# Clustered attention and a rational MoE layer: what the clock-keeping products of TensorE read, and where the float16 identity is formed

## The chip, the cores and the metric

The kernel runs on one core of a Trainium2 chip. The metric is the device time of one execution in microseconds, and less is better. Five engines work side by side, each through a queue of its own in order: PE (TensorE, matrix products), DVE (VectorE), ACT (ScalarE), POOL (GpSimd) and SP (SyncE), whose queue issues the DMA transfers. PEld is the loading of PE's weights, which overlaps its products.

## The reference

For 4 batches of 8 heads with 768 positions of 64 values, q and k are assigned to the nearest of 16 centroids of their head, and attention runs only between positions of one cluster. The attention's output, 3072 rows of 512, goes through a layer with a rational function between two products:

```
q_assign = argmax(q_n . c_n);  k_assign = argmax(k_n . c_n)
scores = where(q_assign == k_assign, scale * q @ k.T, -1e9)
x = softmax(scores) @ v                    # 3072 x 512
h = x @ w_in                               # 512 x 2048
g = (a0 + a1 h + a2 h^2 + a3 h^3) / (1 + |b0| |h| + |b1| h^2 + 1e-6)
out = g @ w_out                            # 2048 x 512
```

## The kernel before

float32 operands are split into a high and a low float16 part, and the products are made of these parts. Per batch the kernel prepares pairs of heads (`prep`), runs the attention (`attend`, for the first pair of the first batch `attend_keys`, which keeps scores transposed), and then the layer (`moe`) over blocks of 256 rows. The weights are loaded and split once, in blocks of 512 columns or rows (`weights`). The work of one batch's attention is interleaved with the layer of the batch before.

Every operation of these functions is first recorded, and then emitted in the order of a long list of numbers in the file (`ORDER`). Within each engine's queue this order stands as it is written. What is not recorded but called directly, the constants at the head of the kernel (L372 to L401), is placed by the framework's scheduler: each engine's queue is filled with what it takes to be ready, so that such an instruction can stand behind recorded ones.

These lines matter here:

- L372 and L373 form `ident`, the float32 identity of 128x128, on GpSimd with `make_identity` (a memset and an affine select). `ones` (L374), `cq`, `tiny`, `up`, `eps` (L387) and `mrow` (L392 to L395) are memsets on DVE, `w16` and `pick` are formed on GpSimd.
- L389 and L390 form `ident16`, the float16 identity, as a cast of `ident` on DVE.
- `warm` (L781 to L788) records one group of eight products of `ident16` with itself into a PSUM tile that nothing reads. `K["warm"]` is 16, so there are 16 such groups; the list puts ten of them at the head of PE's queue, one more ahead of the first real step, and the other five between later steps.
- `prep` works on one pair of heads: ACT sums the squares of k and of q (`sumk`, `sumq`, L409 is the line of every activation), PE transposes the sums into a row (`kt`, `qt`, L1013), DVE takes the maximum (`km`, `qm`, L1015), PE spreads it over the partitions with `ones` (`kb`, `qb`, L1017), DVE makes powers of two of it (`ksc`, `qsc`, L1027 to L1070), ACT scales k and q into float16 (`tk`, `tq`) and DVE forms their low parts (L1089).
- `ident16` is also the identity of the transposes of `tk` and `tq` on PE (L980, the first pair of heads or pairs of the first batch), and of a smaller transpose in `attend_keys` (L1452).
- Loads go through SP's queue in order (L423). A load waits until its buffer's last reader is done: the raw weight blocks (`rwi`, `rwo`) and the first loads of v (`rvm`) share two buffers, k and q (`rk`, `rq`) have their own.

```python
ident16 = cp.tile([P, P], F16, name="ident16")
nc.vector.tensor_copy(out=ident16, in_=ident)
...
def warm(vt):
    wm = misc([P, 2 * TW], F32, f"warm{vt}")
    def spin():
        for _ in range(8):
            nc.tensor.matmul(wm.ap[:, :P], lhsT=ident16, rhs=ident16, start=True, stop=True)
    op("PE", 433, spin, [], [wm], vt)
```

Of the kernel before, what the change touches and what calls it, by code (L numbers as in the profile page):

```python
# [12 lines left out]
BF16 = mybir.dt.bfloat16  # L13
# [5 lines left out]
P = 128  # L19
# [23 lines left out]
class Plan:  # L43
# [5 lines left out]
    def op(self, eng, ns, fn, r=(), w=(), vt=0.0, claim=(), co=(), chain=None, n=None):  # L49
        self.ops.append(fn)  # L50
# [208 lines left out]
def clustered_attention_moe_kernel(  # L259
# [12 lines left out]
    nc = tc.nc  # L272
# [22 lines left out]
    def pool(name, space=None):  # L295
        if name not in pools:
            kw = {} if space is None else {"space": space}
            pools[name] = ctx.enter_context(tc.tile_pool(name=name, bufs=1, **kw))
        return pools[name]

    cp = pool("const")
# [45 lines left out]
    def misc(shape, dt, name):  # L347
        return bank(shape, dt, "m", name, NM)
# [22 lines left out]
    ident = cp.tile([P, P], F32, name="ident")  # L371
# [15 lines left out]
    nc.vector.memset(eps, 1e-9)  # L387

    ident16 = cp.tile([P, P], F16, name="ident16")  # L389
    nc.vector.tensor_copy(out=ident16, in_=ident)  # L390
    mrow = cp.tile([P, NCL], F16, name="mrow")
    nc.vector.memset(mrow, 0.0)  # L392
    nc.vector.memset(mrow[:, 0:8], M_BIG)
# [387 lines left out]
    def warm(vt):  # L781
        wm = misc([P, 2 * TW], F32, f"warm{vt}")

        def spin():
            for _ in range(8):
                nc.tensor.matmul(wm.ap[:, :P], lhsT=ident16, rhs=ident16, start=True, stop=True)

        op("PE", 433, spin, [], [wm], vt)  # L788

# [1064 lines left out]
```

## Time and profile before

| | |
|---|---|
| median of 3 runs | 903.31 us (903.31 to 904.04) |
| the profiled execution | 900.24 us |
| its span, first to last instruction | 898.4 us |
| mean granted TensorE clock | 0.99 of full |
| busy share of PE, DVE, ACT, POOL | 96%, 90%, 88%, 59% |

The rows come from one profiled execution. Times are microseconds from the start of the span, unless marked ns. A row of the timeline gives start, duration, engine, line, operation, what is written and read (a buffer's number is left out, so `ident16` appears as `ident`), how many instructions are merged, and in brackets how long the engine was idle before and what ended that. The chain of work that ended last is followed back from the last instruction, at each step to what released it or to the instruction ahead of it on its engine. The granted clock is 1.00 at 2.4 GHz and 0.50 at 1.2 GHz.

### The profile page before, as it was taken

The page shows a single profiled execution, that of the slowest core. Times are in us where ns is not written, and L with a number is a line of the kernel's source. Part 1 is how long each engine was busy: PE and PEld are TensorE (multiplying, and loading weights), DVE is VectorE, ACT ScalarE, POOL GpSimd, SP SyncE. Part 2 cuts the span into 40 slices and gives each one's busy share as a digit, 9 for nine tenths or more (in the row PEclk, how much of TensorE's full clock was granted, in tenths as well). Part 3 has the DMA queues.
Part 4 walks back from the last instruction along what each step waited for, and adds up shares of the span by engine and source line. Part 5 has one row for each costly group of instructions (what it writes and reads, how often), then busy time and mean ns, then how long its engine had stood idle before and what let it go on. Part 6 is the DMA issues. An engine that isn't in the chain of part 4 may idle for free.

```text
span 898.4 us, 20920 instructions
## 1 busy us (share of the span) xinstructions
PE 862.0 (96%) x7893; PEld 594.4 (66%) x7893; DVE 811.3 (90%) x1610; ACT 794.5 (88%) x1497; POOL 533.2 (59%) x530
## 2 busy tenths in 40 slices
PE   5699999988999999999999999999999999999998
PEld 4566777765666666657667666667676666767654
DVE  3999989789999999989999999999999998877793
ACT  4688899999999999999999999999999999895652
POOL 2337645677766385547556737565666555687664
PEclk9799999999999999999999999999999999999999
DMA  4698876779877999886979999989789875150000
GB/s 155 190 251 216 198 186 144 206 146 210 160 139 139 191 198 183 190 161 127 216 153 167 178 189 171 159 169 179 152 154 170 156 139 95 36 95 1 24 24 24
DMA packets 353013, 135.76 MB, mean 151 GB/s; under 512 B 327824, under 2 KB 344208, under 8 KB 352912
## 3 DMA queue, kind: packets, MB, share of 16 engines
q1 hardware_dynamic: 352912, 134.42, 74.0%
q8 instruction: 62, 1.02, 0.4%
q14 instruction: 39, 0.32, 0.1%
HBM read 41.98 MB, written 6.29 MB: 54 GB/s over the span
## 4 chain that ended last, share of the span: by engine, by line
PE 61%; DVE 17%; ACT 14%; issue 5%; POOL 1%; DMA 1%; SPq 1%; ACTq 0%; DVEq 0%
PE po L1761 20%; PE ph L1612 19%; PE s L1243 7%; PE px L1323 5%; DVE s L1272 3%; ACT s L409 3%; DVE ah L1303 3%; ACT u L409 2%; ACT ah L409 2%; PE s L1386 2%; PE z L1480 2%; PE px L1501 2%; DVE t L1637 1%; DVE t L1630 1%; PE ptl L1138 1%
## 5 line engine op out<-in xcount | busy, mean ns | idle before, releaser
L1612 PE MATMUL ph<-x,win 128*128 128x256 f16 x2304 | 266.2, 273 | 1.1 <-DVE t L1637 0.6
L1761 PE MATMUL po<-wout,g 128*128 128x512 f16 x1152 | 267.1, 379 | 0.0
L1612 PEld LDWEIGHTS <-win 128*128 128x128 f16 x2304 | 223.9, 98 | 42.0 <-DVE t L1637 2.9
L1761 PEld LDWEIGHTS <-g 128*128 128x128 f16 x1152 | 110.5, 98 | 120.1 <-issue 3.4
L1750 POOL TENSOR_TENSOR g<-t,u 128x512 f16<-128x512 f32 x84 | 112.7, 1344 | 93.8 <-DVE t L1743 56.6
L1677 POOL TENSOR_TENSOR s<-s,u 128x512 f32<-128x512 f32 x84 | 111.2, 1329 | 74.9 <-ACT s L409 73.1
L1272 DVE TENSOR_SCALAR_CACHE_REDUCE s<-s,cc 128x768 f32<-128x768 f32 x144 | 144.9, 1018 | 4.4 <-PE s L1243 3.5
L1303 DVE SCALAR_TENSOR_TENSOR ah<-s,su,ah 128x768 f16<-128x768 f32 x144 | 144.1, 1010 | 4.4 <-ACT ah L409 3.9
L409 ACT ACTIVATE ah<-s,su 128x768 f16<-128x768 f32 x144 | 127.8, 899 | 6.6 <-DVE su L1291 6.1
L409 ACT ACTIVATE s<-s,nm 128x768 f32<-128x768 f32 x144 | 125.6, 872 | 8.4 <-DVE s L1272 6.5
L1243 PE MATMUL s<-sk,sq 128*128 128x384 f16 x576 | 115.6, 327 | 6.3 <-DVE ah L1303 5.6
L1243 PEld LDWEIGHTS <-sq 128*128 128x128 f16 x576 | 52.0, 98 | 49.9 <-DVE ah L1303 16.4
L1323 PE MATMUL px<-at,vhi 128*64 128x256 f16 x864 | 73.9, 275 | 1.9 <-DVE s L1731 1.8
L409 ACT ACTIVATE t<-ph,gk 128x512 f32<-128x512 f32 x84 | 65.3, 778 | 0.0
L1630 DVE SCALAR_TENSOR_TENSOR t<-ph,gk,t 128x512 f32<-128x512 f32 x84 | 62.2, 742 | 2.5 <-ACT t L409 1.4
L1637 DVE SCALAR_TENSOR_TENSOR t<-t,gk,ph 128x512 f32<-128x512 f32 x84 | 62.3, 741 | 1.2
L409 ACT ACTIVATE u<-s,cq 128x512 f32<-128x512 f32 x84 | 59.8, 721 | 3.0 <-POOL s L1677 2.9
L409 ACT ACTIVATE s<-u,g 128x512 f32<-128x512 f32 x84 | 60.3, 723 | 0.5
L409 ACT ACTIVATE u<-ph,gk 128x512 f32<-128x512 f32 x84 | 57.7, 688 | 3.3 <-PE ph L1612 3.1
L1731 DVE SCALAR_TENSOR_TENSOR s<-s,g 128x512 f32<-128x512 f32 x84 | 59.8, 714 | 0.5
L1323 PE MATMUL px<-at,vlo 128*64 128x256 f16 x432 | 59.7, 273 | 0.0
L1323 PEld LDWEIGHTS <-vhi 128*64 128x64 f16 x864 | 45.0, 110 | 15.3 <-issue 10.3
(241 smaller groups left out, 1552.4 us busy)
## 6 DMA issues: line engine op xcount, KB each, us to landing
rwi<-in_moe_w_in_dram SPq DMA_DIRECT2D x16, 512.0 KB, 3.9
rwo<-in_moe_w_out_dram SPq DMA_DIRECT2D x16, 512.0 KB, 4.3
rk<-in_k_dram SPq DMA_DIRECT2D x32, 192.0 KB, 3.9
rq<-in_q_dram SPq DMA_DIRECT2D x32, 192.0 KB, 3.7
rvm<-in_v_dram SPq DMA_DIRECT2D x16, 384.0 KB, 4.0
rv<-in_v_dram SPq DMA_DIRECT2D x16, 384.0 KB, 4.1
out_dram<-ob SPq DMA_DIRECT2D x24, 256.0 KB, 2.9
sq<-sq SPq DMA_DIRECT2D x12, 192.0 KB, 4.1
```

Of the source, the lines that this page charges most:

```text
L409: lambda: nc.scalar.activation(out=out(), in_=in_(), func=func, **{a: (x() if callable(x) else x) for a, x in kw.items()}),
L1243: nc.tensor.matmul(sc.ap[:, i, :SH], lhsT=st["q" + x].ap[:, j, t, :], rhs=st["k" + x].ap[:, j, ks, :].rearrange("p t c -> p (t c)"), start ...
L1272: lambda nm=nm, view=view: ts(out=view(), in0=view(), scalar1=cc.ap[:, 0:1], scalar2=None, op0=ALU.mult, op1=ALU.min, accum_out=nm.ap),
L1303: lambda part=part, view=view, su=su: stt(out=part(1), in0=view(), scalar=su.ap, in1=part(0), op0=ALU.mult, op1=ALU.subtract),
L1323: nc.tensor.matmul(px.ap[j * D : (j + 1) * D, :], lhsT=vv.ap[:, j, kt, :], rhs=at[j].ap[:, p_, kt].rearrange("p t c -> p (t c)"), start=(i ...
L1612: nc.tensor.matmul(ph.ap[:, fi * TW : (fi + 1) * TW], lhsT=win[:, wpart, c, f * P : (f + 1) * P], rhs=xs[c].ap[:, xpart], start=(i == 0), ...
L1630: lambda t=t, h=h, ph=ph, col=col: stt(out=t[h].ap, in0=ph.ap, scalar=col("rho")(), in1=t[h].ap, op0=ALU.mult, op1=ALU.mult),
L1637: lambda t=t, h=h, ph=ph, col=col: stt(out=t[h].ap, in0=t[h].ap, scalar=col("a1")(), in1=ph.ap, op0=ALU.add, op1=ALU.mult),
L1677: lambda uv=uv, sv=sv: nc.gpsimd.tensor_tensor(out=sv(), in0=sv(), in1=uv(), op=ALU.mult),
L1731: lambda sv=sv, g16=g16: stt(out=sv(), in0=sv(), scalar=1.0 + 1e-6, in1=g16(0), op0=ALU.add, op1=ALU.mult),
L1750: lambda tv=tv, uv=uv, g16=g16, e=(nc.vector if kshare("gld", b, i_) else nc.gpsimd): e.tensor_tensor(out=g16(1), in0=tv(), in1=uv(), op=A ...
L1761: nc.tensor.matmul(po[ti].ap, lhsT=g16(gg)[:, c0 : c0 + P], rhs=wout[:, wpart, f, :], start=(i == 0 and f == 0), stop=(i == 2 and f == NF ...
```

## The change

The float16 identity is formed directly on GpSimd, with a memset and an affine select of its own, in place of the cast on DVE. A new constant tile of 128x128 bfloat16 ones is set by a memset on DVE, and the groups of eight products read it for both operands. The number, shape and order of the groups stay the same.

```diff
@@ -387,7 +387,9 @@
     nc.vector.memset(eps, 1e-9)
 
     ident16 = cp.tile([P, P], F16, name="ident16")
-    nc.vector.tensor_copy(out=ident16, in_=ident)
+    make_identity(nc, ident16)
+    w16w = cp.tile([P, P], BF16, name="w16w")
+    nc.vector.memset(w16w, 1.0)
     mrow = cp.tile([P, NCL], F16, name="mrow")
@@ -783,7 +785,7 @@
         def spin():
             for _ in range(8):
-                nc.tensor.matmul(wm.ap[:, :P], lhsT=ident16, rhs=ident16, start=True, stop=True)
+                nc.tensor.matmul(wm.ap[:, :P], lhsT=w16w, rhs=w16w, start=True, stop=True)
```

## Rows read from the trace of the kernel before

**Rows 1.** Stretches: length, busy PE, PEld, DVE, ACT, POOL, clock, DMA share, GB/s.

```profile
9.20:15.90 6.70, 6.69 (x89) 6.57 (x89) 0.00 (x0) 1.24 (x5) 2.98 (x4) 1.00 0.27 88
...
45.00:90.00 45.00, 43.91 (x471) 29.91 (x469) 43.02 (x107) 39.35 (x73) 24.40 (x26) 0.98 0.96 232
```

**Rows 2.** The chain that ended last, at its start: start, length, what.

```profile
8.32 0.69 DVE wwo L565
9.01 0.15 DVE ident L390
...
9.21 1.03 PE warm-39.99_113 L786 x8
...
12.78 0.45 PE warm-39.92_156 L786 x8
...
15.46 0.45 PE warm-39.86_234 L786 x8
```

**Rows 3.** DVE's waits from 0 to 45: in total, times, longest.

```profile
DVE km L1015 <- PE kt L1013: 6.9, 1, 6.9
```

**Rows 4.** Timeline, the constants at the head of GpSimd's and DVE's queues.

```profile
0.73 0.20 POOL masks.py:197 MEMSET ident<- 128x128 f32 x1 [0.29 <-POOLq L1838]
...
0.83 0.17 DVE L374 MEMSET ones<- 128x128 f32 x1 [0.83 <-PEq L1838]
...
1.08 0.29 POOL masks.py:199 TENSOR_SCALAR_AFFINE_SELECT ident<-ident 128x128 f32<-128x128 f32 x1
...
1.14 0.06 DVE L387 MEMSET eps<- 128x1 f32 x1
```

**Rows 5.** Timeline, ACT's sums of k and q and what follows them.

```profile
9.02 0.19 ACT L409 ACTIVATION_READ_ACCUMULATOR tk<-rk 128x1 f32 x1
...
10.00 0.19 ACT L409 ACTIVATION_READ_ACCUMULATOR tq<-rq 128x1 f32 x1
...
10.10 0.42 ACT L409 ACTIVATE cn<-cn 128x1 f32<-128x1 f32 x2
```

**Rows 6.** Timeline, first steps behind the constant products on PE and ACT.

```profile
15.75 0.27 PE L1013 MATMUL kt<-ident,sumk 128*1 128x128 f32 x1
...
17.16 0.27 PE L1013 MATMUL qt<-ident,sumq 128*1 128x128 f32 x1
...
17.38 0.94 ACT L409 ACTIVATE tk<-rk,ksc 128x768 f16<-128x768 f32 x1 [6.87 <-DVE ksc L1045]
...
18.23 0.83 ACT L409 ACTIVATE rvm<-rvm 128x768 f32<-128x768 f32 x1
...
19.88 0.66 ACT L409 ACTIVATE mwi<-rwi 128x512 f32<-128x512 f32 x1
```

**Rows 7.** Timeline of SP's queue, two issues of loads.

```profile
6.44 0.39 SPq L423 DMA_DIRECT2D rvm<-in_v_dram  x1
9.08 10.42 SPq L423 DMA_DIRECT2D rwi<-in_moe_w_in_dram  x2
```

**Rows 8.** Stretches of 1.5 us, columns as in rows 1.

```profile
12.00:13.50 1.50, 1.50 (x24) 1.50 (x22) 0.00 (x0) 0.00 (x0) 0.18 (x1) 1.00 0.02 8
...
18.00:19.50 1.50, 0.73 (x10) 0.54 (x9) 1.21 (x6) 1.50 (x4) 0.00 (x0) 0.98 0.00 0
19.50:21.00 1.50, 1.02 (x10) 1.03 (x11) 1.50 (x3) 1.50 (x3) 0.00 (x0) 0.50 0.50 134
...
43.50:45.00 1.50, 1.50 (x32) 1.09 (x31) 1.50 (x3) 0.22 (x1) 1.50 (x2) 0.50 1.05 388
```

**Rows 9.** Timeline, GpSimd's first product.

```profile
9.19 1.27 POOL L574 TENSOR_TENSOR wwo<-wwo,gwo 128x512 f32<-128x512 f32 x1 [6.44 <-DVE ident L390]
```

**Rows 10.** Timeline of PE, three steps at different clocks.

```profile
26.38 0.37 PE L1013 MATMUL kt<-ident,sumk 128*1 128x128 f32 x1
...
41.00 0.81 PE L1386 MATMUL s<-sk,sq 128*128 128x384 f16 x4 [0.47 <-DVE top L1396]
...
43.14 1.27 PE L1386 MATMUL s<-sk,sq 128*128 128x384 f16 x4 [1.33 <-DVE top L1396]
```

## The prediction

> **What bounds the kernel now.** I began with the busy time by stretch [rows 1], whose columns are length, busy time of PE, PEld, DVE, ACT and POOL with instruction counts, granted clock, DMA share and GB/s. In the bulk of the kernel three engines are close to full: of the 45 us from 45 on PE is busy 43.91, DVE 43.02, ACT 39.35, and DMA stands at 0.96. Those stretches are not what the change touches. From 9.20 to 15.90 the picture is another one: PE is busy 6.69 of 6.70 us, while DVE does nothing at all and ACT 1.24 us of work. PE's work there is the constant products.
>
> Next the chain that ended last, at its start [rows 2]. It goes through DVE's L565, then through the cast of the identity (L390, done at 9.16), then through eleven groups of eight constant products, which end at 15.91. So the products are not beside other work here; they are the chain. Nothing reads what they make, but PE takes its queue in order, and behind them stands the first real step, the transpose `kt` of the sums of k (L1013). The waits say the same from the other side [rows 3]: DVE's maximum of that transpose waits 6.9 us for it.
>
> Why do the products begin at 9.21? Not because the identity is late: GpSimd had it finished at 1.08 + 0.29 = 1.37 [rows 4]. The cast stands late in DVE's own queue, right after L565 of the second weight block (8.32 + 0.69 = 9.01), which had waited for a load. DVE's memsets, which need no input, all ran near 1 us [rows 4]. The engine queue is therefore not the order of the program's text, and what has no input goes first.
>
> **The change, part by part.**
> *The products' operand.* They now wait for a memset of 128x128 on DVE instead of the cast. No row shows this memset in bfloat16; the 128x128 float32 one took 0.17 us, the 128x1 one 0.06 [rows 4]. I take 0.17, the nearer in size; the other end makes the sum 0.1 us smaller or nothing. Standing behind the memset of L387 (1.14) it ends at about 1.3. From the cast's end to the first product there were 0.05 us [rows 2], so the products begin at about 1.4 instead of 9.2.
>
> *The products themselves.* Count and shape stay. In the trace four groups ran to 12.78, that is 3.57 us or 0.89 each with the first one's latency, and seven to 15.91, 0.45 each [rows 2]: the half (1.2 GHz) and the full (2.4 GHz) level. (The clock column shows 1.00 for the whole stretch [rows 1]; the groups' length is the better witness.) With the same four and seven they take 6.70 us and end at 8.1. If the clock does not come up at all, eleven take 11 x 0.89 = 9.8 and end at 11.2. That is the bad end.
>
> *What is late next.* `kt` needs the sums of k, which ACT finishes at 9.02 + 0.19 = 9.21 [rows 5]; with the same 0.05 it starts at 9.26. In the trace it starts at 15.75 [rows 6]. The products are over 1.1 us earlier, so **the gain at this point is 15.75 - 9.26 = 6.49 us**, set by ACT's sum and no longer by the products. With the clock never up it is 15.91 - 11.2 = 4.7.
>
> *Does the rest move by the same 6.49?* Everything after `kt` is a chain of queue order and data, so it moves unless it meets something that stays. What stays is what began before 9.2. I check each in turn. `qt` stood at 17.16, moved 10.67; the sums of q are ready at 10.00 + 0.19 [rows 5, 6]. ACT's scaling of k stood at 17.38, moved 10.89; ACT's queue ahead of it ends with the pair of 10.10 at 10.52 [rows 5, 6]. The square of v (18.23, moved 11.74) reads a load issued at 6.44; the weight block of 19.88 (moved 13.39) reads the first of the two issued from 9.08 [rows 6, 7]. DMA was at 0.02 from 12.0 to 13.5 [rows 8], so both had landed by about 12.0; the first of them, issued 2.6 us ahead, surely sooner. Hence no binding there, though only by some 1.4 us for the second. The second load of that pair waits for a buffer which the moved step frees, so it moves too. GpSimd's work from 9.2 to 15.9 is 2.98 us in four instructions [rows 1], over by about 12.3, and its readers on DVE come after 13.
>
> *The identity on GpSimd.* Added: one memset (0.20) and one affine select (0.29) [rows 4]; in float16 they may cost less or somewhat more, and I keep 0.2 to 1 us as bounds. They cost nothing: GpSimd sat idle 6.44 us before 9.19 [rows 9], and the first reader is the transpose of k, which cannot come before 13. If the cover were gone, at most that 1 us would stand before GpSimd's product at 9.19, still off the path.
> *The cast removed.* 0.15 us on the chain [rows 2], already inside the 6.49, because `kt` no longer waits for it.
>
> **Sum.** The profiled execution took 900.24 us (span 898.4 and 1.84 around it), so 900.24 - 6.49 = 893.75. The median of the runs is 903.31, 3.07 above that execution, so on that footing 896.8. That is 0.72%. A measurement of this kernel can tell about 0.2% (1.8 us) from no change.
>
> **The clock afterwards.** Behind the products PE has only sparse work until the attention begins, and the granted clock goes up and down with it. Its price where PE is the bound: four score products (L1386) took 1.27 us at 43.14, where the clock went to half (0.50 in the stretch from 43.50), and 0.81 at 41.00 [rows 8, 10]; and the groups of products took 0.89 against 0.45 [rows 2]; so a microsecond at half does about half a microsecond's work. A move of everything by 6.49 may put such a stretch elsewhere; 3 us of it more or less is about 1.6 us either way. That sets the low end: 896.8 - 1.6 - 0.7 = 894.5, the 0.7 for the spread of the runs (903.31 to 904.04).
> One place is new. In the trace `kt` followed on the products without a gap, and with the sparse work behind it the clock was still at 0.98 from 18.0 to 19.5 and fell to 0.50 only after [rows 8]. Now PE would stand idle from about 8.1 to 9.26, ahead of the same sparse work, the last of which (the q sums) ends near 11.7. If the clock falls in that time, `kt` takes 0.37 us as at 26.38 instead of 0.27 [rows 6, 10], `qt` as much, the group of products between them 0.4 more (0.89 against 0.45), and the two pairs of L1017, by estimate from `kt`, 0.1 each: together 0.8 us on the path to the scaling of q, a gain of 5.7 and a time of 897.6. It is a rival below.
> [...]
>
> **Rivals.**
> *The clock falls in the new gap*, as worked out: 897.6. For it: the idle 1.16 us did not exist before. Against it: the sparse work of 15.9 to 19 had PE waiting too, and the clock held [rows 8].
> *The gain is partly taken back.* A moved step meets one that does not move, most likely a load: DMA is the fullest resource from 45 on (0.96) [rows 1]. For: it has little slack there. Against: loads start when buffers come free, so they move as well, and DMA had almost nothing to do just before (0.02) [rows 8]. With half of the gain gone: 903.31 - 3.2 = 900.1, between 899 and 902.5. The products never reaching the full level belongs here too: 4.7, less 0.8 for the short work at half after it, makes 899.4.
> *Nothing moves.* The memset is queued on DVE where the cast stood, behind L565. Then the products begin at 9.1 and the time is 903.3 less 0.1. Against it: all input-free memsets stand at the head of DVE's queue [rows 4].
> *Slower.* PE now sits idle between the products' end and the dense work for longer, and the clock stays at half into the stretch from 45 on, where PE is busy 43.91 of 45 [rows 1]. At 0.5 us lost per microsecond of half clock the gain is gone after 6.49/0.5 = 13 us of additional half clock there; with 22 us, half of that stretch, it would be 903.31 - 6.49 + 11 = 907.8. Against it: the order of the work behind `kt` is the same as before, and the clock came up in that same sequence.
>
> **Chances.** Forecast as worked out, 894.5 to 899: 0.56. The clock falls in the gap: 0.17, faster as well. Partly taken back: 0.12, of which 0.08 still faster by over 0.2% and 0.04 within. Nothing moves: 0.09. Slower: 0.06. So faster 0.81, same 0.13, slower 0.06. The first two cases lie within 894.5 to 899 and hold 0.73; with most of the third the range is 894.5 to 902.0.
>
> **What would show it.** Right: the first constant product at about 1.4; the groups done before 9; `kt` at about 9.3, waiting for ACT; DVE's wait of 6.9 us shrunk to a fraction; ACT's scaling of k at about 10.9; a span of about 892. The step on the products is wrong if they still begin after 9; the step on the clock if `kt` starts after 10; the step on the move if `kt` is 6.5 earlier and the scores from 45 on are not. The forecast as a whole is wrong if the end moves by less than 4 us.

## The result, and the profile after

The changed kernel took 894.98 us (median of 4 runs, 893.90 to 896.44) against 903.54 us (903.31 to 904.04): a ratio of 0.9906 with a 95% interval of 0.9888 to 0.9923. That is 8.6 us less, where 6.5 was forecast; 894.98 lies inside the range of 894.5 to 902.0, half a microsecond from its low end. The profiled execution after the change took 896.44 us with a span of 894.7, the longest of its four, while the profiled one of before was a short one (900.24). The two spans differ by 3.7 us only. Why three differences, 3.7, 6.5 and 8.6, stand beside each other is what most of the experiments are about.

The timeline of the changed kernel at its start, the lines that answer to [rows 4, 5, 6]:

```profile
1.18 0.17 DVE L392 MEMSET w16w<- 128x128 bf16 x1
...
1.40 1.04 PE L788 MATMUL warm-39.99_118<-w16w 128*128 128x128 bf16 x8 [1.40 <-DVE mrow L394]
...
1.87 0.29 POOL masks.py:199 TENSOR_SCALAR_AFFINE_SELECT ident<-ident 128x128 f16<-128x128 f16 x1
...
8.09 0.61 PE L788 MATMUL warm-39.86_239<-w16w 128*128 128x128 bf16 x8
...
9.18 0.18 ACT L411 ACTIVATION_READ_ACCUMULATOR tk<-rk 128x1 f32 x1
...
9.47 0.27 PE L1015 MATMUL kt<-ident,sumk 128*1 128x128 f32 x1 [0.77 <-issue]
...
11.10 0.94 ACT L411 ACTIVATE tk<-rk,ksc 128x768 f16<-128x768 f32 x1 [0.48 <-DVE ksc L1047]
```

The memset of the ones stands among DVE's other early memsets, took 0.17 us, and the products began at 1.40 instead of 9.21. The last group ended at 8.70, and PE then waited for ACT's sum, which was done at 9.36. The first real step, `kt`, stands at 9.47 where it stood at 15.75.

The chain that ended last, at its start, answers to [rows 2]:

```profile
1.40 1.04 PE warm-39.99_118 L788 x8
...
8.25 0.45 PE warm-39.86_239 L788 x8
8.70 0.77 issue
9.47 0.28 PE kt L1015
```

The product groups are still drawn as the chain, since the step back from `kt` goes to the instruction ahead of it on PE, but 0.77 us of "issue" now stand between them: that is the wait for ACT's sum, which the view does not name. DVE's waits from 0 to 45 answer to [rows 3]: the 6.9 us are down to 0.6.

```profile
DVE km L1017 <- PE kt L1015: 0.6, 1, 0.6
```

The granted clock in the new gap, by stretches (columns as in [rows 1]):

```profile
9.40:11.00 1.60, 1.16 (x12) 0.86 (x12) 0.69 (x4) 1.19 (x4) 1.60 (x3) 1.00 0.52 134
11.00:12.60 1.60, 1.08 (x12) 0.74 (x10) 0.94 (x7) 1.50 (x2) 1.30 (x2) 1.00 0.57 215
12.60:14.20 1.60, 0.50 (x5) 0.51 (x6) 1.60 (x5) 1.49 (x4) 0.00 (x0) 0.59 0.31 56
```

The clock outlived the idle time and the sparse work behind it, and fell only after 12.6.

Further on, two places in the bulk show how much of the 6.28 us is left. First the kernel before, timeline of PE:

```profile
190.38 2.78 PE L1612 MATMUL ph<-x,win 128*128 128x256 f16 x24
...
387.23 0.41 PE L1323 MATMUL px<-at,vhi 128*64 128x256 f16 x4 [1.79 <-DVE s L1731]
```

The same two in the changed kernel:

```profile
184.54 3.95 PE L1614 MATMUL ph<-x,win 128*128 128x256 f16 x24
...
383.43 0.41 PE L1325 MATMUL px<-at,vhi 128*64 128x256 f16 x4 [2.67 <-DVE g L1714]
```

At the first products of the layer 190.38 - 184.54 = 5.84 are left, at the products with v 387.23 - 383.43 = 3.80, and so to the end. The 24 products took 3.95 us instead of 2.78: this execution of the changed kernel had half clock there, the profiled one of before had not. That is 1.17 of the 2.04 us lost between the two places. The other 0.88 are PE's wait ahead of the products with v, 2.67 instead of 1.79, and no half clock: the granted clock is 1.00 around it in both profiles. The view names an instruction of DVE, but that one was done at 382.95; the tile `at` that these products read comes by a DMA transpose, issued at 375.20, and it landed 8.1 us later, just ahead of them, where that of the kernel before (379.86) took 7.3. First the changed kernel, then the kernel before:

```profile
DMA to landing us min/median/max: 8.1/8.1/8.1
```

```profile
DMA to landing us min/median/max: 7.3/7.3/7.3
```

### The profile page after: what moved, and what is told of

Read it like the earlier page. It is cut to its first block, busy times and chain, and to the rows that moved or that the text cites. A ratio compares the mean times of both kernels' runs of the same rounds, so it can differ in the third digit from the quotient of the medians.

```text
span 894.7 us, 20923 instructions
## 1 busy us (share of the span) xinstructions
PE 863.4 (97%) x7893; PEld 595.8 (67%) x7893; DVE 811.5 (91%) x1610; ACT 794.2 (89%) x1497; POOL 534.3 (60%) x532
## 4 chain that ended last, share of the span: by engine, by line
PE 58%; DVE 17%; ACT 15%; issue 5%; DMA 2%; POOL 1%; ACTq 0%; DVEq 0%; SPq 0%
PE po L1763 20%; PE ph L1614 19%; PE s L1245 6%; PE px L1325 5%; ACT s L411 4%; DVE s L1274 3%; DVE ah L1305 3%; ACT u L411 3%; ACT ah L411 2%; PE s L1388 2%; DVE t L1639 1%; DVE t L1632 1%; DMA rwo<-in_moe_w_out_dram 1%; PE px L1503 1%; PE ptl L1140 1%
```

## The experiments

Theory A was that the whole effect is the earlier start of the first real step, with what the products read and where the identity is formed of no account, and that single executions differ by stretches of half clock. Its rivals: the ones themselves help (B), or a second, steady effect (C).

**The same two kernels again.** No edit. The kernel before:

> The unchanged kernel once more, for the spread of its executions. The change moved the first step behind the products by 6.28 us in the two profiles, the ends of the two profiled executions by 3.8, and the medians by 8.6. Theory A (the gain is the earlier start, and single executions differ by stretches of half clock at other places): most executions near 903.5, some near 900; this profile shows kt at 15.7 again, and any difference to the first profile begins at a stretch of half clock. Theory C (the 2.3 us beyond 6.28 are a second, steady effect of the change): the executions stay at 903 to 904 and the profile shows no more half clock than the first one.

The changed kernel, beside it and once more later:

> The changed kernel once more. Theory A: executions between 893 and 897, kt at 9.4 to 9.5, and those profiles that end late have a stretch of half clock of some 3.4 us in the bulk, at about 1 us each. Theory C: always about 895, whatever the clock shows.

> The changed kernel beside them: 893.5 to 896.5, the median 0.3 to 1 us over the one with the products in the waits (theory A), or the same as that (theory C).

The kernel before gave 901.82 us (12 runs, 899.70 to 904.21; 0.9996 [0.9985, 1.0007] of itself). The changed one gave 893.90 (893.60 to 894.86; 0.9913 [0.9899, 0.9927]) and 893.83 (892.89 to 894.80; 0.9913 [0.9901, 0.9926]). Over all runs, 67 executions of the kernel before have a median of 902.12 (899.62 to 904.93) and 14 of the changed one 894.07 (892.89 to 896.44): the effect is 8.05 us, and single executions of one kernel spread over 4 to 5 us. So comparing two profiled executions, 3.7 us apart here, says little. Two expectations were missed: most executions of the kernel before lie near 902 and not near 903.5, so the first four were long ones, and `kt` stood at 15.31 in its second profile, not at 15.7.

Where one such difference arises is seen in the stretch of the first products of the layer. In order: the first profile of the changed kernel, its second one, and the second profile of the kernel before, where the same work stands near 189:

```profile
183.40:186.40 3.00, 3.00 (x58) 2.46 (x55) 2.59 (x9) 3.00 (x10) 0.86 (x3) 0.53 0.79 220
```

```profile
183.40:186.40 3.00, 3.00 (x63) 2.78 (x59) 2.66 (x9) 3.00 (x9) 0.93 (x3) 1.00 0.78 218
```

```profile
189.20:192.20 3.00, 3.00 (x57) 2.44 (x54) 2.61 (x9) 3.00 (x9) 0.88 (x3) 0.54 0.79 219
```

Same kernel, same work, 0.53 or 1.00. Each time PE had waited about 1.4 us just before, for the maxima of v. A stretch of half clock follows this wait in some executions of either kernel and not in others. It is not the only source of the spread. The second profile of the changed kernel was the longest of its four (894.86) and had full clock here; it lost 0.7 us at the products with v, where the transpose of `at` took 7.8 us to land. In the other profiles of these two kernels it took 7.2 (the second of before) and 7.4 (the third of the changed one).

**The identity on GpSimd, the products late.**

```diff
-    w16w = cp.tile([P, P], BF16, name="w16w")
-    nc.vector.memset(w16w, 1.0)
+    w16w = cp.tile([P, P], F16, name="w16w")
+    nc.vector.tensor_copy(out=w16w, in_=ident)
```

> The float16 identity stays on GpSimd, but the products read a cast that DVE makes of the float32 identity, as before. Theory A (start time alone): products from about 9.2, kt at 15.7, 903.5 us within 0.2%, no gain at all. Rival (the identity on GpSimd, or DVE freed of the cast's reader, brings part): up to 1 us below 903.5.

901.50 us (898.81 to 902.55; 0.9991 [0.9981, 1.0001]). The timeline of PE:

```profile
9.43 1.03 PE L788 MATMUL warm-39.99_118<-w16w 128*128 128x128 f16 x8 [9.43 <-DVE w16w L392]
...
16.27 0.27 PE L1015 MATMUL kt<-ident,sumk 128*1 128x128 f32 x1
```

With the cast back in front of the products the gain is gone. Forming the float16 identity on GpSimd brings nothing by itself that can be told from noise.

**The products read the identity that GpSimd forms.**

```diff
-    w16w = cp.tile([P, P], BF16, name="w16w")
-    nc.vector.memset(w16w, 1.0)
...
-                nc.tensor.matmul(wm.ap[:, :P], lhsT=w16w, rhs=w16w, start=True, stop=True)
+                nc.tensor.matmul(wm.ap[:, :P], lhsT=ident16, rhs=ident16, start=True, stop=True)
```

> The products read the float16 identity that GpSimd forms; there is no tile of ones. Theory A: products from about 2.2 us, still done before ACT's sum of k, so kt at 9.4 to 9.5 and 895 us within 0.2%, the same as the change. Theory B (ones keep the clock up better than an identity): later rise of the clock or more half clock, kt later than 9.6, and 1 us or more above the change.

895.94 us (894.13 to 896.77; 0.9933 [0.9920, 0.9947], beside 0.9913 [0.9899, 0.9927] of the changed kernel run with it). The timeline of PE:

```profile
2.23 1.03 PE L786 MATMUL warm-39.99_116<-ident 128*128 128x128 f16 x8 [2.23 <-POOL ident masks.py:199]
...
7.32 0.89 PE L786 MATMUL warm-39.93_177<-ident 128*128 128x128 f16 x8
...
9.84 0.27 PE L1013 MATMUL kt<-ident,sumk 128*1 128x128 f32 x1
```

Most of the gain is there without any ones. The expected equality was missed in part: six groups and some of the seventh ran at half, and the products, begun 0.83 us later, ended at 10.00, behind ACT's sum (9.48). So in this profile they were on the path again, by some 0.3 us. These are theory B's signs: a late rise of the clock, `kt` behind 9.6, a median 2 us above the change. But the late rise is not the identity's: with the ones, in the second profile of the changed kernel with filled waits (shown further on), six groups and part of the seventh ran at half as well, and behind casts of the identity it was some four:

```profile
6.50 0.74 PE L788 MATMUL warm-39.93_179<-w16w 128*128 128x128 bf16 x8
```

The 2 us between the two medians are more than that 0.3, and this profile was itself the shortest of its executions (894.13); the intervals overlap only from 0.9920 to 0.9927, and whether the ones do anything beyond the earlier start is not settled by it.

**The ones alone.**

```diff
-    make_identity(nc, ident16)
+    nc.vector.tensor_copy(out=ident16, in_=ident)
```

> The products read the tile of ones; the float16 identity is cast by DVE again. Theory A: products from 1.4 us, kt at 9.4 to 9.5, the same time as the change within 0.2% (the cast stands behind L567 on DVE and ends by 9.5, its reader comes at 13). Rival (the identity's place matters): 0.5 us or more above the change.

896.09 us (4 runs, 894.40 to 896.98; 0.9931 [0.9909, 0.9952]). The cast is back on DVE, but nothing waits for it:

```profile
9.03 0.22 DVE L390 CAST ident<-ident 128x128 f16<-128x128 f32 x1
9.73 0.28 DVE L1017 TENSOR_REDUCE km<-kt 1x1 f32<-1x128 f32 x1 [0.48 <-PE kt L1015]
```

`kt` stood at 9.42, as in the changed kernel. The profile shows no cost of the cast. By the median the rival's mark, 0.5 us or more above the change, was met; but these are four runs with a spread of 2.6 us, and the changed kernel was not run beside them. Whether the place of the identity is worth anything stays open. That the ones are there and the median is no better than with the identity as operand (895.94) gives theory B no support.

**No products ahead of the first step.** Eleven of the 16 groups are left out; they compute nothing that is used.

```diff
+    EARLY = {-40 + 0.01 * i for i in (1, 13, 0, 10, 8, 12, 7, 6, 15, 11, 14)}
...
-            for _ in range(8):
+            for _ in range(0 if vt in EARLY else 8):
```

> The changed kernel without the eleven groups of constant products ahead of the first step; the five later ones stay. Theory A (the step behind them now waits for ACT's sum, so the products are off the path and only keep the clock up for the short steps that follow): the transpose of k's sums again at 9.4 to 9.5 but at half clock, q's scaling 0.8 us later, 895 to 895.5 us, still 7 us under the kernel before. Rival (their clock is still worth having until the dense work): half clock longer, 897 us or more.

894.85 us (893.21 to 897.83; 0.9919 [0.9895, 0.9942]). The timeline of PE, at half clock by the lengths (`kt` takes 0.37 us instead of 0.27):

```profile
9.72 0.37 PE L1017 MATMUL kt<-ident,sumk 128*1 128x128 f32 x1 [9.72 <-ACT tk L411]
...
11.80 0.42 PE L1017 MATMUL qt<-ident,sumq 128*1 128x128 f32 x1
```

Here the view names the wait outright: `kt` was released by ACT's sum. From `kt` to ACT's scaling of q it took 14.04 - 9.72 = 4.32 us, in the changed kernel 12.77 - 9.47 = 3.30. So the eleven groups are worth 1.0 us on this path, against 0.8 forecast for a clock that falls early. Nearly the whole gain of the change would have come from leaving them out.

This profile was one of the long executions (897.22). Behind the wait for the maxima of v, 2.2 us here, the clock stood at 0.50 from 184.4 to 191.2, and the 24 products took 4.78 us instead of 2.78:

```profile
187.06 4.78 PE L1616 MATMUL ph<-x,win 128*128 128x256 f16 x24
```

**The loads of k and q first.** The list of the order was changed at its head (shown here as one line before and one after); of the 16 groups five stay ahead of the first step, four stand between the steps behind it, three where they were, and four are left out.

```diff
-4438 4450 40 41 42 43 4437 4447 4445 4449 4444 4443 4452 4448 44 3 4 74 75 5 6 76 77 78 79 386 387 389 4451 391 392 393 398 399 400 4446 385 384 390 394 395 396 397 401 402 403 404 4439 7 8 405 406 413 407 411 45 12 13 408 409 416
+4438 4450 40 41 42 43 4437 4447 4445 44 3 386 387 389 385 384 390 74 4 5 6 391 392 393 398 399 400 4449 394 395 396 397 401 402 403 404 4439 4444 4443 405 75 78 7 8 406 413 76 77 407 79 411 45 12 13 408 409 416 4452 4448 4451 4446
...
+    LEFT = {-40 + 0.01 * i for i in (9, 11, 14, 15)}
...
-            for _ in range(8):
+            for _ in range(0 if vt in LEFT else 8):
```

> The changed kernel with the loads of k and q issued ahead of the first block of w_out, ACT's sums of k and q and their chain ahead of that block's steps, five groups of products ahead of the first step, three more behind it, four before the second pair, four left out. Theory A (ACT's sum of k, waiting behind the weight block, is what bounds the start now): the first step at about 6.6 instead of 9.45, and 1.5 to 2.5 us less than the change (about 892.5), as the weight block comes 1 to 1.5 us later and takes some of it back. Rival (the start is bound elsewhere, by the weight blocks' buffers): the first step moves, the time stays within 0.5 us of the change or rises.

896.09 us (894.89 to 896.79; 0.9932 [0.9914, 0.9949]). The rival's number came: the first step moved and the time rose. In its timeline (line numbers stand 192 lower, since the list takes fewer lines):

```profile
7.01 0.84 ACT L219 ACTIVATE tk<-rk 128x768 bf16<-128x768 f32 x1 [1.44 <-DMA rk<-in_k_dram]
...
8.05 0.29 PE L825 MATMUL kt<-ident,sumk 128*1 128x128 f32 x1 [2.66 <-issue]
...
13.07 0.92 ACT L219 ACTIVATE tq<-rq,qsc 128x768 f16<-128x768 f32 x1
```

`kt` came 1.4 us earlier, not 2.8, because ACT's sum now waits for the load of k itself. ACT's scaling of q came at 13.07, no earlier than with the change (12.77). Two things held it up that the edit brought along. With five groups ahead, PE stood idle for 2.66 us before `kt`, and behind that idle time the clock was at half:

```profile
9.60:11.20 1.60, 1.23 (x10) 0.83 (x7) 0.52 (x3) 1.23 (x2) 0.00 (x0) 0.50 0.02 6
```

And the factor for q was ready at 12.25, but ACT's steps for the weight block, moved behind the sums (from 10.81 on), had pushed the square of v back, and the scaling stands behind that in ACT's queue. So this run does not tell what the loads alone would have given. ACT's waits from 0 to 50 for the blocks of w_in grew to 6.3 us, where the changed kernel has 2.3 from 0 to 45; this kernel first, then the changed one:

```profile
ACT mwi L219 <- DMA rwi<-in_moe_w_in_dram: 6.3, 2, 4.0
```

```profile
ACT mwi L411 <- DMA rwi<-in_moe_w_in_dram: 2.3, 1, 2.3
```

**Products in two waits of the bulk.** The first edit fills the wait for the maxima of v of the second batch, the second that ahead of the products with v near 383; the tiles written are overwritten by the real product right after.

```diff
-        op("PE", 300, lambda: nc.tensor.transpose(out=pt.ap[0:1, :], in_=vm1.ap, identity=ident), [vm1], [pt], vt)
...
+        def largest():
+            for _ in range(16 if b == 1 else 0):
+                nc.tensor.matmul(pt.ap, lhsT=w16w, rhs=w16w, start=True, stop=True)
+            nc.tensor.transpose(out=pt.ap[0:1, :], in_=vm1.ap, identity=ident)
...
+        op("PE", 300, largest, [vm1], [pt], vt)
...
+            for _ in range(24 if (n, tb, k0) == ("1_3", 1, 0) else 0):
+                nc.tensor.matmul(px.ap[:, :P], lhsT=w16w, rhs=w16w, start=True, stop=True)
```

> The changed kernel with constant products put into two waits of PE in the bulk: 16 ahead of the transpose of the maxima of v of the second batch (near 181 us) and 24 ahead of the products with v near 383. Theory A (the executions differ by stretches of half clock of 3.4 us behind these two waits, at 1 to 1.5 us each): none of them in the profile, the slowest executions gone, the median 0 to 0.8 us lower than the change. Rival (the spread has another cause): the same spread, and up to 1 us longer where the products are not hidden.

> The changed kernel with the products in the two waits, once more beside the others: 893 to 894.5, no half clock behind the two waits. If it was luck, a spread up to 896.5 as for the change.

893.64 us (892.79 to 894.44; 0.9906 [0.9888, 0.9925]) and 893.45 (892.89 to 894.55; 0.9911 [0.9899, 0.9923], beside 0.9913 [0.9901, 0.9926] of the changed kernel). PE's waits in the two places in the changed kernel:

```profile
PE vt L816 <- DVE vm L814: 1.4, 1, 1.4
```

```profile
PE px L1325 <- DVE g L1714: 2.7, 1, 2.7
```

And with the products in them the first is 0.5, the second gone from the list, and the stretch behind the first at full clock:

```profile
PE vt L820 <- DVE vm L814: 0.5, 1, 0.5
```

```profile
184.00:187.00 3.00, 3.00 (x63) 2.79 (x60) 2.66 (x9) 3.00 (x9) 0.94 (x3) 1.00 0.79 219
```

The ten executions end between 892.79 and 894.55, those of the changed kernel between 892.89 and 896.44: the longest are not seen. The median moves by 0.4 to 0.5 us, which the intervals do not separate. It is no proven improvement. In the second place PE waits for the transpose of `at`, and the filler only keeps it busy meanwhile. Half clock behind that place was seen in one profile, that of the late products, from 389.0 to 392.4.

The same on the kernel before, with its identity as the operand:

> The kernel before with the constant products (of the identity) in the same two waits of PE in the bulk. Theory A (the 1.5 to 2 us by which the medians differ beyond the 6.3 of the start come from half-clock stretches behind those waits, which hit the timed executions of the kernel before more often): no such stretch in the profile, a median near 900.2, 1.5 to 2 us under the kernel before, and 6.3 to 6.8 over the changed kernel with the same products. Theory C (the change has a second, steady effect elsewhere): the median stays at 902 within 0.7 us, 8 over.

900.81 us (898.90 to 903.91; 0.9987 [0.9976, 0.9998]), so 1.26 less than the kernel before beside it (902.07). That is between the two theories (1.5 to 2 less, or 0.7 at most), and its interval, 0.2 to 2.2 us, leaves room for both. Above the changed kernel with the same products it lies by 900.81 - 893.45 = 7.4 us, where theory A had 6.3 to 6.8 and theory C 8. The profiled execution was the longest, 903.91, and shows a third place. Stretches 47 to 50 of this kernel, then of the kernel before:

```profile
47.00:50.00 3.00, 3.00 (x32) 2.32 (x29) 2.34 (x6) 2.35 (x6) 1.27 (x2) 0.50 0.95 309
```

```profile
47.00:50.00 3.00, 3.00 (x32) 2.09 (x30) 2.52 (x10) 2.30 (x7) 1.30 (x2) 1.00 0.87 246
```

In the attention of the first batch the clock stayed at half for longer, which no edit here touched. Half clock somewhere between 38 and 51 is common: 8 of the 14 profiles have it, the first of the kernel before and the second and third of the changed one among them. It is not the whole of this execution's delay either: another 1.0 us was lost near 126, at a clock of 1.00, where PE waited for ACT and ACT for the load of a block of w_out.

And without the early products, but with those in the waits (the two edits together):

> No products ahead of the first step, but those in the two waits. Theory A: the early products are worth the 0.8 us of short steps at full clock and nothing else, so 0.5 to 1 us over the kernel with the waits filled, 894 to 895, and without the slow executions (up to 897.8) of the kernel without early products. Rival: the slow ones stay, since half clock from the start is what costs.

894.94 us (893.99 to 895.48; 0.9923 [0.9911, 0.9935]). The long executions of the kernel without early products (up to 897.83) are not seen in these five, as theory A has it, and the median is 1.5 over the kernel with both, rather than 0.5 to 1. `kt` to the scaling of q took 8.98 to 13.29, 4.31 us again.

## Why the prediction was right

**What bounds, and the start of the products: right.** Products at 1.40 as forecast, the memset 0.17 as taken, the cast off the path. They ended at 8.70 instead of 8.1, since five groups and part of a sixth ran at half and not four; this cost nothing, because ACT's sum came later still. Putting the products back behind a late cast brings the time of before back.

**What is late next: right, 0.2 us off.** `kt` at 9.47 instead of 9.26, since the second weight block's activations began at 7.31 in this execution and ACT's sum ended at 9.36. The kernel without early products names ACT's sum as what releases `kt`. Here are `kt` and its first product, the first group at 1.4 or 9.4, in ten profiles:

| profile | first product | kt | products to kt |
|---|---|---|---|
| before, first and second | 9.21, 9.01 | 15.75, 15.31 | 6.54, 6.30 |
| products late; before with filled waits | 9.43, 9.71 | 16.27, 16.45 | 6.84, 6.74 |
| changed, three profiles | 1.40 | 9.47, 9.43, 9.24 | ended before it |
| ones alone; filled waits, two profiles | 1.40 | 9.42; 9.85, 9.35 | ended before it |

The means of `kt` are 15.95 and 9.46: 6.49 us, the number of the forecast. To the digit this is chance: with the two profiles of the kernel before and the three of the changed one alone it is 15.53 - 9.38 = 6.15.

**The rest moves by the same: right at the start, blurred later.** 6.28 at `kt` and 5.84 at the layer's first products in the two first profiles, then 3.80: 1.17 us went to half clock that the execution of before did not meet, 0.88 to a DMA transpose that landed later. By the prediction's own sign, wrong if the end moves by less than 4 us, these two executions (900.24 and 896.44) would have called it wrong; the medians do not, and the sign was too fine for single executions.

**The sum was a little too small.** The step that failed is the one that set the sum against a single execution ("With the same four and seven they take 6.70 us") and moved it to the median unchanged. Before the change the products were on the chain, so the time at which the clock comes up was too, and it differs from execution to execution: 6.30 to 6.84 us of products in the table, 7.61 with the identity of GpSimd. After the change it is hidden behind ACT's sum. Against 8.05 us between the pooled medians the start accounts for some 6.2 to 6.5, and 1.5 us or more are left open. Filling the two waits narrows the difference to 7.4 us, from 902.07 - 893.83 = 8.2 in the runs beside it, but each of these medians is known to about 1 us only, so it is not shown that the rest lies in half clock there. Nor does the kernel before show more half clock on the whole: the mean granted clock is recorded for each execution, and its median is 0.990 for either kernel (63 and 14 executions). That is a coarse measure, since it includes the sparse work of the start. The third place, near 38 to 51, was not tested, and waits for loads and transposes differ between executions too, by about 1 us. Theory C, a second, steady effect, is therefore not ruled out.

**Luck in the number.** The range was set from 903.31, the median of three executions that were long ones, and took 0.7 us for their spread; 67 executions have a median of 902.12 and spread over 5.3 us. The first median of the changed kernel fell inside the range, the next two, 893.90 and 893.83, lie below its low end of 894.5. As a difference the range reached down to 8.8 us of gain, and the 8.05 lies within that.

**The rivals.** The clock did not fall in the new gap before `kt` in any profile with all eleven groups ahead of it, where PE was idle for up to 1.5 us; with five groups and 2.66 us it did. The price set on it, 0.8, was measured by leaving the products out, 1.0. The Trainium skill, "TensorE: Matmul & The Clock Gate", section "HAM oscillation — how this bites in real kernels", tells of a kernel whose PE waits for loads, each time for longer than its bursts of about 2 us, and starts each burst at half clock. The wait of 2.66 us agrees with it (0.50 behind it). The shorter waits here are not what it tells of: behind 0.77 us at the start the clock stayed at 1.00 until 12.6, behind 1.4 us in the bulk it was 0.53 in some executions and 1.00 in others. The gain was not taken back by loads at the start, but the kernel with the loads of k and q in front shows the rival's mechanism: there the weight blocks came late, and with the half clock gave back more than was won. Whether the transpose of `at` lands later because of the change (8.1, 7.8 and 7.4 us in three profiles, against 7.3 and 7.2 in two of the kernel before) is open. Half clock that costs more than the gain was not seen; the largest single cost was 2.0 us for the 24 products, in the kernel without early products (4.78 against 2.78), and 1.2 in the changed kernel (3.95).

## What to carry to other kernels

Work that nothing reads still holds up what stands behind it in an in-order queue: look whether filler that keeps a clock up is itself the chain, and give it an operand that waits for nothing. When an early stretch is freed, find at once what releases the next step, because moving that too may only uncover a load, as with the loads of k and q in front. And size a change against several executions: here single ones of the same kernel lie 4 to 5 us apart, more than half of the gain.

## What the runs showed of the hardware that was not expected

A transpose by DMA of the same shape took from 5.6 us (with the waits filled) to 8.1 us to land, and PE's products followed it. The same row of product groups reached the full clock after four groups in one execution and after nearly seven in another (12.60 in the first profile of before, 7.32 into the seventh with GpSimd's identity). One identical stretch of work ran at 0.53 or 1.00 of the clock after the same wait of 1.4 us, at a cost of 1.17 us for 24 products. Products of an identity and of ones took the same 0.85 us a group at half and 0.45 at full.
